# Attention's decay matrices from two triangle scans and a product of two factors, in a fused mLSTM, MoE and MLP kernel on one core

## The chip, the core and the metric

The kernel runs on one core of a Trainium2 chip. A core has five engines, each with an instruction queue of its own, worked off in order: TensorE (PE, with its weight load PEld), VectorE (DVE), ScalarE (ACT), GpSimd (POOL) and SyncE (SP, which here issues DMAs). SBUF is the on-chip memory of 128 partitions, PSUM the accumulators that PE writes. The metric is the device time of one execution in microseconds; lower is better.

## The reference

Three layers follow each other. The first is a gated linear attention (mLSTM) over 4 batches, 8 heads, 768 tokens and a head size of 40; its output, 3072 tokens of 320 values, goes through a mixture of 8 experts with one expert per token, and then through a dense layer of 2048.

```python
for t in range(S):
    m_new = np.maximum(f_gate[:, :, t] + m, i_gate[:, :, t])
    f_stab = np.exp(f_gate[:, :, t] + m - m_new)
    i_stab = np.exp(i_gate[:, :, t] - m_new)
    C = f_stab[:, :, None, None] * C + i_stab[:, :, None, None] * np.einsum('bhd,bhe->bhde', vt, kt)
    n = f_stab[:, :, None] * n + i_stab[:, :, None] * kt
    y[:, :, t] = o * np.einsum('bhde,bhe->bhd', C, qt) / np.maximum(np.abs(nq), 1.0)
```

Only the attention is touched. Over a chunk of tokens it equals a product of scores with a decay matrix whose element (s, t) is the product of `f_stab` from s+1 to t, for s up to t, and zero below.

## The kernel before

The attention is cut into 24 units: 6 chunks of 128 tokens, and in each chunk the 4 batches; unit u is batch u % 4 of chunk u // 4. For every unit and all 8 heads together the kernel builds the decay matrix `pm` (128 source tokens in the partitions, 8 x 128 target tokens in the columns). `fload` (L264) brings the gates of the unit's 8 heads to all partitions with one broadcast DMA from a buffer in DRAM, `scan` (L358) runs one DVE scan over 1024 columns that multiplies by the gates and adds an identity. PE computes the scores (`scores_mm`, L392), DVE multiplies them with `pm` into `wm` (`scores_w`, L402), PE multiplies `wm` with the weighted values (`pv`, L453) and the query with the running state (`inter`, L438), and updates the state (`state`, L407) from keys that POOL weighs with the last column of `pm` (`kweigh`, L383). `epilogue1` and `epilogue2` (DVE) and `finish` (POOL) make the unit's output `x`. Each `pv` pass writes 128 columns, of which the next head overwrites 64, so only 41 per head are used.

The units are pipelined by hand: the loop from L829 on issues, for each u, pieces of several units in a fixed order, and each engine's queue takes them in that order. In iteration u stand, one after the other: `finish(u-2)`, `fload(u+2)`, `scores_mm(u)`, `state_up(u-1)`, `epilogue1(u-1)`, `scan(u+1)`, ranks of a routing batch, `scores_w(u)`, halves of expert weights that are split for later (from u = 10 or 11 on), `pv(u-1)`, `epilogue2(u-1)`, `vprime(u+1)`, `kweigh(u+1)`, the transposes of the output of unit u-2 (`route_t`), `sigm`, `state(u)`, `inter(u)`, the router's logits of unit u-2 (`route_l`, whose last step is a copy on DVE), every fourth unit the router's choice (`route_hot`, five DVE steps), one unit later its counts (`route_cnt`), `state_decay(u)`, scatters of finished rows (POOL; one from u = 10, two from u = 19), and the loads for unit u+3. The scores have one PSUM buffer `sp`, so `scores_mm(u+1)` waits until `scores_w(u)` has read it. `route_t` and a few others share two PSUM buffers named `pt`.

The gates are prepared with 32 partitions (batch and head) by 768 tokens: `gates_m` to `gates_e` (L273 to L317) for chunks 0 and 1 before the loop, and for chunks 2 to 5 spread over units 0 to 5; `put_dec` writes them to DRAM for the broadcasts. `gates_e` makes `est`, the products up to a chunk's last token, which `gates_pe` transposes at unit 5.

Of the kernel before, what the change touches and what calls it, by code (L numbers as in the profile page):

```python
# [9 lines left out]
F32 = mybir.dt.float32  # L10
# [16 lines left out]
def kernel(ctx, tc, qT_in, kT_in, kvo_in, i_gate, f_gate, expert_emb, tau, w12, wio, out, dbg=None):  # L27
# [113 lines left out]
    with ExitStack() as actx:  # L141
# [53 lines left out]
        nc.vector.tensor_copy(ident_h, ident.unsqueeze(1).to_broadcast([P, H, P]))  # L195
        tri = ap1.tile([P, P], F32, name="tri")
# [48 lines left out]
        mm = ap1.tile([BH, S + 1], F32, name="mm")  # L245
# [12 lines left out]
        dec = [dram.tile([n, BH, P], F32, name=f"dec{i}") for i, n in enumerate((2, NCH - 2))]  # L258

        def put_dec(i):  # L260
            c0, c1 = (0, 2) if i == 0 else (2, NCH)
            nc.sync.dma_start(out=dec[i].rearrange("c k t -> k c t"), in_=fz[:, c0:c1])

        def fload(u):  # L264
            b, c = units[u]
            fb[u] = wk.tile([P, H, P], F32, tag="fb", name="fb")
            src = dec[0][c] if c < 2 else dec[1][c - 2]
            src = src[b * H:(b + 1) * H].rearrange("h t -> (h t)").unsqueeze(0)
            nc.sync.dma_start(out=fb[u].rearrange("p h t -> p (h t)"), in_=src.to_broadcast([P, H * P]))
# [1361 lines left out]
```

## Time and profile before

| | |
|---|---|
| three runs | 756.64, 758.26 (median), 759.30 us |
| the profiled execution | 759.01 us, span of its instructions 757.3 us |
| busy over the span | PE 712.0 us (94%), PEld 669.0, DVE 538.7 (71%), ACT 345.2 (46%), POOL 232.4 (31%) |
| granted TensorE clock | 0.99 of full speed over the span |
| attention loop | about the first 180 us; the experts and the dense layer follow |

The page cuts the span into 40 slices of 19 us and gives the busy tenths of each engine: DVE is at 7 to 9 in slices 1 to 11, which are the attention, and at 4 to 7 behind them, where PE is at 9 throughout. The shares of the whole span are an average over stages with different limits.

### The profile page before, as it was taken

Reading aid. Unit: us, or ns where it says so; the run is one execution under the profiler, and the core shown is the slowest. Engines: PE = TensorE matmul, PEld = TensorE weight load, DVE = VectorE, ACT = ScalarE, POOL = GpSimd, SP = SyncE. Lnnn points to the kernel's source line nnn. Section 1 sums busy time; section 2 is a strip of 40 time slices with the busy share of each in tenths; the row PEclk is TensorE's granted clock in tenths of the full one; section 3 lists DMA queues with packets and bytes.
Section 4 is the critical chain, followed back from the end, with each engine's and each line's share of the span. In section 5 each row is a group of like instructions: output and inputs, shape, how many; then the busy total and the mean of one; then the engine's idle time right before and its main releaser. Section 6 shows DMA issues by size and latency. Waiting matters only on the chain.

```text
span 757.3 us, 13220 instructions
## 1 busy us (share of the span) xinstructions
PE 712.0 (94%) x4708; PEld 669.0 (88%) x4708; DVE 538.7 (71%) x1082; ACT 345.2 (46%) x806; POOL 232.4 (31%) x346
## 2 busy tenths in 40 slices
PE   7697888878999999999999999999999999999995
PEld 6697888878888999999998888998889988899994
DVE  7889999998499989898976765544544554445542
ACT  4344243332566666676645443333333343334442
POOL 4563476785343333455401003003003003002011
PEclk9889999999999999999999999999999999999998
DMA  6979887672559777877732121211211101101000
GB/s 188 314 244 300 265 268 237 205 256 77 165 198 234 234 203 188 233 209 232 250 82 80 27 59 46 42 33 40 40 41 36 37 26 35 43 1 46 11 19 18
DMA packets 69913, 99.57 MB, mean 131 GB/s; under 512 B 31218, under 2 KB 56082, under 8 KB 69842
## 3 DMA queue, kind: packets, MB, share of 16 engines
q1 hardware_dynamic: 66770, 90.79, 40.6%
q0 software_dynamic: 3072, 7.89, 2.9%
q8 instruction: 38, 0.62, 0.3%
q14 instruction: 33, 0.27, 0.1%
HBM read 77.53 MB, written 17.19 MB: 125 GB/s over the span
## 4 chain that ended last, share of the span: by engine, by line
issue 42%; PE 23%; POOL 5%; DVE 2%; DMA 1%; ACT 0%; POOLq 0%; SPq 0%; ACTq 0%
PE acc L1131 12%; PE hp L138 10%; POOL out_dram L1176 3%; POOL xr L1282 2%; PE xt L1055 1%; DMA xr<-y 1%; DVE w L121 0%; POOL gap L1178 0%; DVE hs L1105 0%; DVE xl L1057 0%; DVE w L111 0%; DVE fr L1200 0%; POOLq L1626 0%; DVE xl L1073 0%; ACT hs L1444 0%
## 5 line engine op out<-in xcount | busy, mean ns | idle before, releaser
L1131 PE MATMUL acc<-wout,hhl 128*128 128x320 f32 x1152 | 187.0, 309 | 0.0
L1131 PEld LDWEIGHTS acc<-wout,hhl 128*128 128x128 f32 x1152 | 175.9, 188 | 7.4
L1116 DVE TENSOR_TENSOR sg<-hp,sg 128x512 f32<-128x512 f32 (+1 forms) x112 | 68.8, 614 | 93.5 <-ACT sg L1115 93.1
L138 PE MATMUL hp<-xh,win 128*128 128x512 f32 (+1 forms) x560 | 131.0, 364 | 0.0
L1118 DVE TENSOR_TENSOR hhl<-sg,hhl 128x512 fp32r<-128x512 f32 (+1 forms) x112 | 71.3, 637 | 70.2 <-ACT hhl L1117 70.2
L1176 POOL DMA_INDIRECT out_dram<-o,tokd x24 | 24.0, 1001 | 312.4 <-ACT o L1160 308.7
L1115 ACT ACTIVATE sg<-hp 128x512 f32<-128x512 f32 (+1 forms) x112 | 60.4, 539 | 124.6 <-PE hp L138 124.6
L1131 PE MATMUL acc<-w,hs 128*128 128x320 f32 x636 | 104.9, 310 | 2.0 <-ACT hs L1104 1.0
L138 PEld LDWEIGHTS hp<-xh,win 128*128 128x128 f32 x560 | 93.9, 188 | 11.5 <-ACT xh L1321 0.2
L1131 PEld LDWEIGHTS acc<-w,hs 128*128 128x128 f32 x636 | 96.8, 188 | 4.4 <-DVE hs L1105 1.9
L1117 ACT CAST hhl<-sg 128x512 fp32r<-128x512 f32 (+1 forms) x112 | 62.6, 559 | 80.1 <-DVE sg L1116 80.1
L138 PE MATMUL hp<-xl,win 128*128 128x512 f32 (+1 forms) x336 | 85.7, 363 | 0.0
L110 POOL TENSOR_TENSOR w<-r,w 128x256 fp32r<-128x256 f32 x58 | 47.7, 824 | 106.6 <-ACT w L105 94.2
L138 PEld LDWEIGHTS hp<-xl,win 128*128 128x128 f32 x336 | 58.8, 189 | 10.9 <-DVE xl L1322 0.2
L138 PE MATMUL hp<-xh,w 128*128 128x440 f32 (+6 forms) x320 | 66.8, 338 | 0.0
L400 PE MATMUL sp<-qT,kblk 120*128 120x128 f32 x384 | 51.9, 292 | 11.9 <-DVE wm L405 11.9
L400 PEld LDWEIGHTS sp<-qT,kblk 120*128 120x128 f32 x384 | 48.2, 204 | 16.7 <-DVE wm L405 14.6
L360 DVE TENSOR_TENSOR_SCAN pm<-fb,ident_h 128x1024 f32<-128x1024 f32 x23 | 57.3, 2492 | 5.2 <-DMA fb<-dec 2.0
L138 PEld LDWEIGHTS hp<-xh,w 128*128 128x128 f32 x320 | 51.4, 189 | 1.7
L1104 ACT ACTIVATE hs<-hp 128x440 fp32r<-128x440 f32 (+6 forms) x64 | 30.2, 472 | 41.5 <-PE hp L138 40.1
L463 PE MATMUL op<-vp_in,wm 128*128 128x128 f32 (+1 forms) x368 | 44.6, 275 | 0.0
L463 PEld LDWEIGHTS op<-vp_in,wm 128*128 128x128 f32 x368 | 43.5, 194 | 0.0
(304 smaller groups left out, 1082.8 us busy)
## 6 DMA issues: line engine op xcount, KB each, us to landing
r<-in_w_dram SPq DMA_DIRECT2D x32, 704.0 KB
fb<-dec SPq DMA_DIRECT2D x23, 512.0 KB
kvo<-in_kvo_dram SPq DMA_DIRECT2D x24, 480.0 KB
c<-in_wio_dram SPq DMA_DIRECT2D x16, 704.0 KB
rows<-zt SPq DMA_DIRECT2D x8, 640.0 KB
qT<-in_qT_dram SPq DMA_DIRECT2D x24, 180.0 KB
xr<-y SPq DMA_DIRECT2D x5, 640.0 KB
kblk<-in_kT_dram SPq DMA_DIRECT2D x48, 60.0 KB
```

The lines of the kernel that those rows point to most:

```text
L110: eng.tensor_tensor(out=t[:, 3 * P:5 * P].rearrange("p (c f) -> p c f", c=2), in0=r1[:, 0:2], in1=hif[:, 0:2], op=ALU.subtract)
L138: nc.tensor.matmul(hp, a, b, start=(i == 0), stop=(i == len(seq) - 1))
L360: nc.vector.tensor_tensor_scan(out=pm[u].rearrange("p h t -> p (h t)"), data0=fb[u].rearrange("p h t -> p (h t)"), data1=ident_h.rearrange ...
L400: nc.tensor.matmul(sp[:, h - hs.start], kblk[u % NLD][0:KR, h // 3, h % 3, :], qT[u][0:KR, h // 3, :], start=True, stop=True)
L463: nc.tensor.matmul(ops[:, h * NW:h * NW + n], wm[u][:, h], vp_in[u % NLD][:, h * DV:h * DV + n], start=True, stop=True)
L1104: nc.scalar.activation(out=hh, in_=hp, func=AF.Relu)
L1115: nc.scalar.activation(out=sg, in_=hp, func=AF.Sigmoid, scale=1.702)
L1116: nc.vector.tensor_tensor(out=g, in0=hp, in1=sg, op=ALU.mult)
L1117: nc.scalar.copy(hh, g)
L1118: nc.vector.tensor_tensor(out=hl, in0=g, in1=hh.bitcast(F32), op=ALU.subtract)
L1131: nc.tensor.matmul(acc_t[blk][i], hl if j == 2 else hh, w[:, DM:2 * DM] if j == 1 else w[:, 0:DM], start=(first and j == 0), stop=(last an ...
L1176: sc = nc.gpsimd.indirect_dma_start(out=out, out_offset=bass.IndirectOffsetOnAxis(ap=tokd[:, ti:ti + 1], axis=0), in_=o[:, i], in_offset=None)
```

## The change

From chunk 2 on (units 8 to 23) a decay matrix is made of three parts: two triangles of 64x64 tokens for each head, and the square between them. The triangles come from one DVE scan over 512 columns, in which partitions 0 to 63 hold the gates of a chunk's first half and partitions 64 to 127 those of its second half, loaded by two broadcasts of half the width. The scan writes a PSUM buffer `pt`; ACT copies the upper triangle to `pm`. The square is, for each head, an outer product: the products of gates from a source token to the end of the first half, times those from the start of the second half to the target token. `far_mm` forms it for all heads with one PE product over 96 rows, into the upper half of the same PSUM buffer, and `far_out` copies square and lower triangle to `pm` with one ACT copy of 512 columns. `kweigh(u+1)` moves behind `far_out(u+1)` for these units.

The factors are made once for chunks 2 to 5: `factors` inside `gates_e` and `suffix` at the end of iteration 4 (six doubling steps on DVE), `spread_b` and `spread_a` in iterations 5 and 6 (12 ACT products that place each head's or batch's rows among zeros), `masks` in iteration 1. Each factor is split into a rounded part and a rest, which is why the gates lie three times in the partitions: 96 rows, loaded by six DMAs in place of two. `pv` writes 96 columns per pass in place of 128, for all units. The two `pm` buffers become fixed tiles, and an early buffer of the experts takes a `wm` buffer instead.

```diff
-        ig = ap1.tile([BH, S], F32, name="ig")
-        fg = ap1.tile([BH, S], F32, name="fg")
-        nc.sync.dma_start(out=fg, in_=f_gate.rearrange("b h s -> (b h) s"))
-        nc.sync.dma_start(out=ig, in_=i_gate.rearrange("b h s -> (b h) s"))
+        R3, HP, CH = 3 * BH, P // 2, 2
+        ig = ap1.tile([R3, S], F32, name="ig")
+        fg = ap1.tile([R3, S], F32, name="fg")
+        for t, g in ((fg, f_gate), (ig, i_gate)):
+            for a in range(3):
+                nc.sync.dma_start(out=t[a * BH:(a + 1) * BH], in_=g.rearrange("b h s -> (b h) s"))
...
+        id2 = ap1.tile([P, H, HP], F32, name="id2")
+        hmask = ap1.tile([R3, H], F32, name="hmask")
+        bmask = ap1.tile([R3, B], F32, name="bmask")
+        fac = {n: ap1.tile([R3, NCH - CH, HP], F32R, name=n) for n in ("fa", "fb")}
+        facA = ap1.tile([R3, NCH - CH, HP], F32, name="facA")
+        lhsA = ap1.tile([R3, B, NCH - CH, HP], F32R, name="lhsA")
+        rhsB = ap1.tile([R3, NCH - CH, H, HP], F32R, name="rhsB")
+        pmb = [ap1.tile([P, H, P], F32, name=f"pmb{i}") for i in range(2)]
...
-        mm = ap1.tile([BH, S + 1], F32, name="mm")
+        mm = ap1.tile([R3, S + 1], F32, name="mm")
...
-        dec = [dram.tile([n, BH, P], F32, name=f"dec{i}") for i, n in enumerate((2, NCH - 2))]
+        dec = [dram.tile([CH, BH, P], F32, name="dec0"), dram.tile([2 * (NCH - CH), BH, HP], F32, name="dec1")]
...
+            if i == 0:
+                nc.sync.dma_start(out=dec[0].rearrange("c k t -> k c t"), in_=fz[0:BH, 0:CH])
+            else:
+                nc.sync.dma_start(out=dec[1].rearrange("c k t -> k c t"),
+                                  in_=fz[0:BH, CH:NCH].rearrange("k c (a t) -> k (c a) t", t=HP))
...
+            fb[u] = wk.tile([P, H, P], F32, tag="fb", name="fb").rearrange("p h t -> p (h t)")
+            if c < CH:
+                src = dec[0][c, b * H:(b + 1) * H].rearrange("h t -> (h t)").unsqueeze(0)
+                nc.sync.dma_start(out=fb[u], in_=src.to_broadcast([P, H * P]))
+            else:
+                fb[u] = fb[u][:, 0:H * HP]
+                for a in range(2):
+                    src = dec[1][2 * (c - CH) + a, b * H:(b + 1) * H].rearrange("h t -> (h t)").unsqueeze(0)
+                    nc.sync.dma_start(out=fb[u][a * HP:(a + 1) * HP], in_=src.to_broadcast([HP, H * HP]))
...
+            if c0 >= CH:
+                at = lambda t: t.rearrange("k c (a t) -> k c a t", t=HP)[:, c0:c1, :, 0:1]
+                nc.vector.tensor_copy(at(fd), at(fz))
+                nc.vector.memset(at(fz), 0.0)
+                return
...
         def gates_e(c0, c1):
 
             nc.vector.tensor_tensor_scan(out=fl(est, c0, c1), data0=fl(fz, c0, c1), data1=fl(fd, c0, c1), initial=0.0,
                                          op0=ALU.mult, op1=ALU.add)
             n = c1 - c0
+            if c0 >= CH:
+                factors()
             gd = wk.tile([BH, n, B * G], F32, tag="gd", name="gd")
             gd_t[c0] = gd
             nc.vector.tensor_tensor(out=gd, in0=pairm.unsqueeze(1).to_broadcast([BH, n, B * G]),
-                                    in1=est[:, c0:c1, P - 1:P].to_broadcast([BH, n, B * G]), op=ALU.mult)
+                                    in1=est[0:BH, c0:c1, P - 1:P].to_broadcast([BH, n, B * G]), op=ALU.mult)
...
+        def masks():
+
+            v = ident[0:R3, 0:R3].rearrange("k (a b h) -> k a b h", b=B, h=H)
+            nc.vector.tensor_reduce(out=hmask, in_=ident[0:R3, 0:R3].rearrange("k (a h) -> k h a", h=H), axis=AX.X, op=ALU.add)
+            nc.vector.tensor_reduce(out=bmask, in_=v.rearrange("k a b h -> k b a h"), axis=AX.XY, op=ALU.add)
+            for a in range(2):
+                nc.vector.tensor_copy(id2[a * HP:(a + 1) * HP],
+                                      ident[a * HP:(a + 1) * HP, a * HP:(a + 1) * HP].unsqueeze(1).to_broadcast([HP, H, HP]))
+
+        def suffix():
+
+            nc.vector.memset(facA[:, :, HP - 1:HP], 1.0)
+            nc.vector.tensor_copy(facA[:, :, 0:HP - 1], fz[:, CH:NCH, 1:HP])
+            k = 1
+            while k < HP:
+                nc.vector.tensor_tensor(out=facA[:, :, 0:HP - k], in0=facA[:, :, 0:HP - k], in1=facA[:, :, k:HP], op=ALU.mult)
+                k *= 2
+            nc.scalar.copy(fac["fa"], facA)
+            lo = slice(BH, 2 * BH)
+            nc.vector.tensor_tensor(out=fac["fa"][lo], in0=facA[lo], in1=fac["fa"][lo].bitcast(F32), op=ALU.subtract)
+
+        def factors():
+
+            late = est[:, CH:NCH, HP:P]
+            nc.scalar.copy(fac["fb"], late)
+            lo = slice(2 * BH, R3)
+            nc.vector.tensor_tensor(out=fac["fb"][lo], in0=late[lo], in1=fac["fb"][lo].bitcast(F32), op=ALU.subtract)
+            nc.vector.tensor_tensor(out=late, in0=late, in1=est[:, CH:NCH, HP - 1:HP].to_broadcast([R3, NCH - CH, HP]), op=ALU.mult)
+
+        def spread_a():
+            for b in range(B):
+                nc.scalar.mul(lhsA[:, b], fac["fa"].bitcast(F32), bmask[:, b:b + 1])
+
+        def spread_b(h0, h1):
+            for h in range(h0, h1):
+                nc.scalar.mul(rhsB[:, :, h], fac["fb"].bitcast(F32), hmask[:, h:h + 1])
...
         def scan(u):
-            pm[u] = wk.tile([P, H, P], F32, tag="pm", name="pm")
-            nc.vector.tensor_tensor_scan(out=pm[u].rearrange("p h t -> p (h t)"), data0=fb[u].rearrange("p h t -> p (h t)"),
+            pm[u] = pmb[u % 2]
+            if units[u][1] >= CH:
+                t = tri_t[u] = ps_t.tile([P, H, HP], F32, tag="pt", name="tri")
+                nc.vector.tensor_tensor_scan(out=t.rearrange("p h t -> p (h t)"), data0=fb[u], data1=id2.rearrange("p h t -> p (h t)"),
+                                             initial=0.0, op0=ALU.mult, op1=ALU.add)
+                nc.scalar.copy(pm[u][0:HP, :, 0:HP], t[0:HP])
+                return
+            nc.vector.tensor_tensor_scan(out=pm[u].rearrange("p h t -> p (h t)"), data0=fb[u],
                                          data1=ident_h.rearrange("p h t -> p (h t)"), initial=0.0, op0=ALU.mult, op1=ALU.add)
 
+        tri_t = {}
+
+        def far_mm(u):
+            b, c = units[u]
+            if c >= CH:
+                nc.tensor.matmul(tri_t[u][0:HP].rearrange("p h t -> p (h t)"), lhsA[:, b, c - CH],
+                                 rhsB[:, c - CH].rearrange("k h t -> k (h t)"), start=True, stop=True)
+
+        def far_out(u):
+            if units[u][1] >= CH:
+                nc.scalar.copy(pm[u][:, :, HP:P], tri_t.pop(u))
...
-                n = min(2, H - h) * NW
+                n = NW + NW // 2 if h < H - 1 else NW
                 nc.tensor.matmul(ops[:, h * NW:h * NW + n], wm[u][:, h], vp_in[u % NLD][:, h * DV:h * DV + n], start=True, stop=True)
...
-                for n, tag in (("h", "fb"), ("l", "pm")):
+                for n, tag in (("h", "fb"), ("l", "wm")):
...
                 if ok(u - 1):
                     pv(u - 1)
                     epilogue2(u - 1)
+                if ok(u + 1):
+                    far_mm(u + 1)
                 if u == 5:
                     gates_pe(2, NCH)
+                    spread_b(0, H // 2)
+                if u == 6:
+                    spread_b(H // 2, H)
+                    spread_a()
+                if u == 1:
+                    masks()
                 if ok(u + 1):
                     vprime(u + 1)
-                    kweigh(u + 1)
+                    if units[u + 1][1] < CH:
+                        kweigh(u + 1)
...
+                if ok(u + 1) and units[u + 1][1] >= CH:
+                    far_out(u + 1)
+                    kweigh(u + 1)
...
                     gates_e(2, NCH)
                     sigm(u)
+                    suffix()
```

## Rows read from the trace of the kernel before

**Rows 1.** busy time by stretch: us, then PE, PEld, DVE, ACT, POOL, PEclk, DMA, GB/s
```profile
64.60:93.60 29.00, 25.22 (x224) 24.28 (x224) 27.85 (x65) 9.63 (x34) 12.65 (x18) 1.00 0.83 269
93.60:122.70 29.10, 25.07 (x224) 24.20 (x223) 28.36 (x60) 10.75 (x37) 20.17 (x25) 1.00 0.74 238
122.70:151.80 29.10, 24.79 (x221) 23.92 (x220) 28.36 (x60) 10.76 (x37) 20.17 (x25) 1.00 0.75 235
151.80:173.60 21.80, 16.29 (x144) 15.50 (x143) 21.23 (x39) 6.09 (x21) 19.60 (x23) 1.00 0.67 229
```

**Rows 2.** timeline of DVE, one plain interval: start us, us, engine, line, operation
```profile
129.41 2.78 DVE L360 TENSOR_TENSOR_SCAN pm<-fb,ident_h 128x1024 f32<-128x1024 f32 x1
132.12 1.19 DVE L405 TENSOR_TENSOR wm<-sp,pm 128x1024 f32<-128x1024 f32 x1
...
134.76 0.12 DVE L542 COPY logit_all<-r 128x8 f32<-128x8 f32 x1
134.79 0.85 DVE L435 SCALAR_TENSOR_TENSOR Cst<-dC,mask,Cst 120x123 f32<-120x123 f32 x3
...
135.96 2.79 DVE L360 TENSOR_TENSOR_SCAN pm<-fb,ident_h 128x1024 f32<-128x1024 f32 x1
```

**Rows 3.** timeline of PE, the same stretch; in brackets idle before, releaser
```profile
130.12 0.31 PE L507 MATMUL pr<-ident,x 128*128 128x128 f32 x1
...
130.49 0.73 PE L414 MATMUL dC<-vp_in,kw 128*120 128x123 f32 x6
131.06 0.83 PE L450 MATMUL ip<-Cst,qT 120*128 120x123 f32 x6
...
132.21 0.39 PE L540 MATMUL r<-enT,xT 128*128 128x128 f32 x2
133.36 2.05 PE L400 MATMUL sp<-qT,kblk 120*128 120x128 f32 x16 [0.77 <-DVE wm L405]
```

**Rows 4.** groups by line, DVE, up to 60 us: xcount | busy us, mean ns
```profile
L373 DVE TENSOR_TENSOR_SCAN pm<-f,ident_h 128x512 f32<-128x512 f32 x2 | 2.3, 1194 | 0.0
```

**Rows 5.** groups by line, ACT, whole run, one shape
```profile
L1104 ACT ACTIVATE hs<-hp 128x512 fp32r<-128x512 f32 x8 | 4.8, 598 | 8.1 <-PE hp L138 8.1
```

**Rows 6.** timeline of PE in the last part: passes of 256 columns
```profile
702.23 0.75 PE L138 MATMUL hp<-xh,win 128*128 128x256 f32 x5
702.82 0.52 PE L138 MATMUL hp<-xl,win 128*128 128x256 f32 x3
```

**Rows 7.** timeline of ACT, the stretch of group 2
```profile
130.69 0.48 ACT L511 COPY xT<-pr 128x384 f32<-128x384 f32 x1 [4.58 <-PE pr L509]
```

**Rows 8.** timeline of POOL, the stretch of group 2
```profile
129.25 0.81 POOL L501 TENSOR_TENSOR x<-num,sg 128x320 f32<-128x320 f32 x1
130.01 2.71 POOL L380 TENSOR_TENSOR vp_in<-kvo,ei_tok 128x320 f32<-128x320 f32 x1
132.68 0.73 POOL L387 TENSOR_TENSOR kw<-kvo,pm 128x320 f32<-128x320 f32 x1
133.56 1.07 POOL L616 DMA_INDIRECT rows<-x,slot_i  x1 [0.16 <-issue]
```

**Rows 9.** timeline of DVE: a routing choice, from its first step to the step behind
```profile
83.90 0.19 DVE L560 TENSOR_REDUCE mx<-logit_all 128x4 f32<-128x32 f32 x1
...
85.61 0.84 DVE L435 SCALAR_TENSOR_TENSOR Cst<-dC,mask,Cst 120x123 f32<-120x123 f32 x3
```

**Rows 10.** groups by line, DVE, 64.6 to 173.6 us
```profile
L598 DVE TENSOR_TENSOR cnt<-cnt,cs 128x8 bf16<-128x8 bf16 x4 | 2.9, 713 | 0.1
```

**Rows 11.** timeline of SP: one DMA issue
```profile
1.28 0.41 SPq L156 DMA_DIRECT2D ig<-in_i_gate_dram  x1
```

**Rows 12.** groups by line, DVE, 90 to 245 us, a product of 192 columns
```profile
L1243 DVE TENSOR_TENSOR t<-logit_all,rn 128x192 f32<-128x192 f32 x1 | 0.4, 357 | 0.0
```

**Rows 13.** timeline of DVE: the scan of unit 7
```profile
56.13 2.29 DVE L360 TENSOR_TENSOR_SCAN pm<-fb,ident_h 128x1024 f32<-128x1024 f32 x1 [1.30 <-POOL vp_in L380]
```

**Rows 14.** timeline of PE: the scores of unit 4
```profile
37.29 3.79 PE L400 MATMUL sp<-qT,kblk 120*128 120x128 f32 x16 [3.33 <-DVE wm L405]
```

More of the change, by code (lines that the diff above doesn't have):

```diff
@@ L248 @@
         nc.vector.memset(f0, 0.0)
-        fd = ap1.tile([BH, NCH, P], F32, name="fd")
+        fd = ap1.tile([R3, NCH, P], F32, name="fd")
         nc.gpsimd.memset(fd, 0.0)
-        est = ap1.tile([BH, NCH, P], F32, name="est")
+        est = ap1.tile([R3, NCH, P], F32, name="est")
         fz = fg.rearrange("k (c t) -> k c t", t=P)
@@ L256 @@
         gd_t = {}
-        dec = [dram.tile([n, BH, P], F32, name=f"dec{i}") for i, n in enumerate((2, NCH - 2))]
+        dec = [dram.tile([CH, BH, P], F32, name="dec0"), dram.tile([2 * (NCH - CH), BH, HP], F32, name="dec1")]
         def put_dec(i):
-            c0, c1 = (0, 2) if i == 0 else (2, NCH)
-            nc.sync.dma_start(out=dec[i].rearrange("c k t -> k c t"), in_=fz[:, c0:c1])
+            if i == 0:
[3 more added lines that the diff above has]
+                                  in_=fz[0:BH, CH:NCH].rearrange("k c (a t) -> k (c a) t", t=HP))
         def fload(u):
             b, c = units[u]
[L266 to L269, printed above, removed]
+            fb[u] = wk.tile([P, H, P], F32, tag="fb", name="fb").rearrange("p h t -> p (h t)")
[7 more added lines that the diff above has]
+                    nc.sync.dma_start(out=fb[u][a * HP:(a + 1) * HP], in_=src.to_broadcast([HP, H * HP]))
         fl = lambda t, c0, c1: t[:, c0:c1].rearrange("k c t -> k (c t)")
@@ L306, in gates_z @@
             if c0 == 0:
-                nc.vector.tensor_copy(f0[0:BH], fz[:, 0])
+                nc.vector.tensor_copy(f0[0:BH], fz[0:BH, 0])
         def gates_e(c0, c1):
@@ L323, in gates_pe @@
             for i in range(n):
-                nc.tensor.transpose(pg[:, 2 * i * BH:(2 * i + 1) * BH], ist[:, c0 + i], ident[0:BH, 0:BH])
-                nc.tensor.transpose(pg[:, (2 * i + 1) * BH:(2 * i + 2) * BH], est[:, c0 + i], ident[0:BH, 0:BH])
+                nc.tensor.transpose(pg[:, 2 * i * BH:(2 * i + 1) * BH], ist[0:BH, c0 + i], ident[0:BH, 0:BH])
+                nc.tensor.transpose(pg[:, (2 * i + 1) * BH:(2 * i + 2) * BH], est[0:BH, c0 + i], ident[0:BH, 0:BH])
             g0 = 2 * n * BH
@@ L358, in scan @@
         def scan(u):
-            pm[u] = wk.tile([P, H, P], F32, tag="pm", name="pm")
-            nc.vector.tensor_tensor_scan(out=pm[u].rearrange("p h t -> p (h t)"), data0=fb[u].rearrange("p h t -> p (h t)"),
-                                         data1=ident_h.rearrange("p h t -> p (h t)"), initial=0.0, op0=ALU.mult, op1=ALU.add)
+            pm[u] = pmb[u % 2]
[6 more added lines that the diff above has]
+            nc.vector.tensor_tensor_scan(out=pm[u].rearrange("p h t -> p (h t)"), data0=fb[u],
+                                         data1=ident_h.rearrange("p h t -> p (h t)"), initial=0.0, op0=ALU.mult, op1=ALU.add)
+        tri_t = {}
[7 more added lines that the diff above has]
+                nc.scalar.copy(pm[u][:, :, HP:P], tri_t.pop(u))
         def scan0(j):
             if j == 0:
-                pm[0] = wk.tile([P, H, P], F32, tag="pm", name="pm")
+                pm[0] = pmb[0]
             n = H // 2
```

## Prediction

> **What bounds the kernel now.** I began with the 40 slices of the page, to see where VectorE (DVE) is full: in the attention loop, and not behind it. Then I cut the loop at the starts of its scans [rows 1]. The 16 units from chunk 2 on are units 8 to 23; between the scan of unit 8 (64.6 us) and that of unit 23 (173.6 us) lie 15 intervals, 29.0, 29.1 and 29.1 us for four units each and 21.8 us for the last three. DVE is busy 27.9 to 28.4 of each 29 us, TensorE (PE) some 25, ScalarE (ACT) 10 to 11. So DVE sets the pace there. One plain interval shows it: from scan to scan 6.55 us, without a gap on DVE [rows 2], while PE's next scores wait 0.77 us for DVE's product `wm` [rows 3], which leaves PE with 6.55 - 0.77 = 5.78 us of work. Everything behind the loop follows the loop's end, so a microsecond there is a microsecond of the total.
>
> **The change in the loop.** Removed from DVE: a full scan, 2.78 us in the unit shown [rows 2], becomes one of half the length. A scan of 128x512 took 1.19 us [rows 4]; it read PSUM and wrote SBUF, the new one does the reverse, and I take the same. DVE's plain interval falls to about 6.55 - (2.78 - 1.19) = 4.96 us, so DVE no longer sets the pace. The load of `fb` is halved too; it has landed long before it is used in these units, so I count nothing.
>
> Added: on ACT two copies out of PSUM of 512 columns, 0.60 us each [rows 5]; ACT has 18 us of 29 free. On PE one product of 512 columns: five of 256 columns start within 0.59 us [rows 6], 0.12 each, so 0.23. PE gets time back, since `pv` multiplies 96 columns in place of 128 in 14 of its 16 passes: the six state passes (four of 123 columns, two of 82) take 0.57 us from their start to the next step's, the transposes of 128 columns about 0.11 each [rows 3], so a pass of 82 costs about 0.07 and one of 96 about 0.08; 14 x 0.03 = 0.4. PE's own work becomes 5.78 + 0.23 - 0.4 = 5.6 us.
>
> What matters more is a new ring. `far_mm(u+1)` stands in PE's queue before `route_t`, and waits for ACT's first copy, which waits for the scan of u+1; behind it on PE wait the transposes, `state`, `inter` and `route_l`; DVE's copy of the logits waits for `route_l`, and the next scan is queued behind that copy, `state_up` and `epilogue1`. Before, the scan was followed by nothing that PE waited for at once. Its length: `route_t` to the end of `route_l`, 130.12 to 132.60, is 2.48 [rows 3]; logits copy to scan, 134.76 to 135.96, is 1.20 [rows 2]; scan 1.19; copy 0.60; product 0.23; three hand-overs of 0.05 (as `wm`'s end, 133.31, to the scores at 133.36) 0.15. Sum 5.85 us.
>
> GpSimd (POOL) has a ring as well, because `kweigh(u+1)` now waits for ACT's second copy. From `route_t`: the copy of `xT` starts 0.57 later and takes 0.48 [rows 7], then the second copy 0.60, so `kweigh` starts at about 1.75 and takes 0.73; the scatter and what lies around it 1.3; then the two products of `finish` begin at about 3.8, just when the scan does (2.48 + 0.05 + 1.20 = 3.73). A scan and a product of POOL, both of which read SBUF, did not run together: a product that began inside a scan took 2.71 us, the one ahead of it 0.81, and it ended 0.5 us after the scan [rows 8]. If the first product is ahead, the scan starts up to 0.6 us late and the ring is 6.3 to 6.45; if the scan is ahead, `x` is ready 1.19 + 1.6 us after 3.73, at 6.5, and `route_t` waits for it. Bounds 5.85 and 6.55; I take 6.4, nearer the upper end, as two of the three cases lie there.
>
> The Trainium skill, "SBUF — State Buffer", section "Who interferes with whom", says of a DVE instruction with two inputs in SBUF and a GpSimd instruction that reads SBUF that whoever is first holds the shared port for its whole instruction, and the other stops. The 2.71 us agree. By that rule a plain interval would be 6.3 to 6.55; if the two shared the port's bandwidth without stopping it would be about 5.85.
>
> The 15 intervals then: a plain unit 6.4 (6.55 before). A unit with the routing's choice carries 1.71 us more on DVE inside the ring [rows 9], so 5.85 + 1.71, about 7.5; it has no port conflict left, since the scan comes after `finish`. A unit with counts carries up to 0.2 + 0.71 [rows 10], so 6.7. Four units: 2 x 6.4 + 7.5 + 6.7 = 27.0, against 29.1: 2.1 saved, twice, 4.2. The first four (29.0) hold one more chain of small steps on DVE, the choice of the first expert, and less plain work of DVE, as no weights are split there yet: the ring gives least there, I take 0.5 (0 to 1.5). In the last three units (21.8) there is no state: the ring loses 0.57 of PE and some 0.8 of DVE (`state_up` [rows 2]) and PE's work falls to 5.0; POOL, with two scatters, 1.6 + 0.7 + 2.6 = 4.9, up to 6.1 where the scan stands between. I take 6.0, 5.6 and 6.8 (choice): 18.4, so 3.4 saved (2 to 5). Unit 23's own shorter scan: 1.1 at most, as half of it goes, PE busy beside it, 0.5. Sum of gains 8.6 us (5 to 12).
>
> **The change ahead of the loop.** Six loads of the gates in place of two: four more issues on SP of 0.41 us [rows 11], so 1.6 us later for the first gates and for the first q, k and v; queued behind them is all that SP issues at the start. Some of it is taken up where SP waits for the gates anyway: 0 to 1.6, I take 0.9. Gates on 96 partitions in place of 32 cost no more per instruction, as their columns are the same. `masks` at unit 1 is four small instructions, about 1.1 us of DVE; unit 4's scan waits for data later anyway; I take 0.2 (0 to 1.1).
>
> `factors` and `suffix` at unit 4 stand in DVE's queue before `state_up(4)`, `epilogue1(4)`, `scores_w(5)` and the scan of unit 6, all of which shift by as much. Nine operations of up to 256 columns, by the row of 192 columns (0.357 us [rows 12]) 0.3 to 0.45 each and 3.4 together, small ones 0.2, and two waits for ACT's copies of the factors, about 0.5 each: 4.6 us (3.0 to 5.5). Before the scan of unit 7 DVE idles 1.30 us now [rows 13]; that swallows as much. So 3.3 less a little that PE's order gives back, 3.1 (1.5 to 4.2). ACT's twelve products for `rhsB` and `lhsA` fall into units 5 and 6, where PE waits for DVE by then: nothing. Sum of losses 4.2 us (2 to 7).
>
> While DVE works on this, PE idles about 2.4 us before `inter(5)`. An idle stretch of 3.33 us before the scores of unit 4 was followed by 16 passes in 3.79 us, not 2.05 [rows 14, 3]: 1.7 us lost. No row shows whether 2.4 us is enough for that; 0 to 1.7 is in the range. [...]
>
> **Sum.** The profiled execution took 759.01 us (span 757.3 and 1.7 around it). 759.0 - 8.6 + 4.2 = 754.6. The median of the runs, 758.26, lies 0.75 below the profiled one, so I predict 753.9 us.
>
> **Rivals.** (1) The port is not in the way: plain units 5.85, in all about 3.5 us less, 750.4. For it: the two starts lie 0.1 us apart, and any shift parts them. Against: POOL's work and the scan still add up inside one interval.
> (2) No change that can be measured: the loop gives only 7 us, and the early block takes 6.5, by full start delay and the half clock above; about 758. For it: the only gap of DVE in the stretch that could take up the new work is that of 1.30 us.
> (3) Slower: POOL does both products of `finish` ahead of the scan. The scan then starts at 3.8 + 1.6 = 5.4 after `route_t`, and the ring is 5.4 + 1.19 + 0.6 + 0.23 + 0.1 = 7.5. Four plain units lose 1.1 each against my 6.4, three with counts 0.7, two of the last 0.8: 8.1, so 762. It decides from a mean interval 0.3 us (4.4 / 15) above my figures. For it: the tie; against: after the first product the scan has waited longer.
> (4) The scan into PSUM takes nearly as long as the full one: 1.1 us more in the ring; about 765. Only the 1.19 us stand against it.
>
> **Chances.** Mine 0.48 (its own range 750 to 757), (1) 0.15, (2) 0.20, (3) 0.14, (4) 0.03. About 0.3% (2.3 us) is what this kernel's runs can tell from no change, so faster is below 756.0, slower above 760.5. Faster: 0.43 of mine, all of (1), 0.03 of (2): 0.61. Same: 0.05 and 0.15: 0.20. Slower: (3), (4) and 0.02: 0.19. The range 748 to 761 leaves out the lower half of (1), and most of (3) and (4).
>
> **What would show it.** A half scan of 1.2 us; plain intervals of 6.3 to 6.5 with PE waiting for ACT before `far_mm`, and DVE with gaps before the logits copy; choice units near 7.5; unit 7's scan 2 to 4 us later than 56.1. I am wrong if DVE is still without gaps, if the scans are 7 us apart or 5.9, or if the early units lose over 7 us.

## The result and the profile after

The changed kernel takes 764.88 us (median of four runs, 764.27 to 767.43) where the kernel before takes 758.35 beside it: a ratio of 1.0095 (95% interval 1.0066 to 1.0124), 6.5 us slower. 753.9 was predicted, with 748 to 761 as the range, so it lies outside, on the slower side. The profiled execution is the one of 767.43 us, with a span of 765.7; most of its excess over the median is a stretch at the lower clock, priced below.

The same cuts as in [rows 1], in the profile after, from the scan of unit 8 to that of unit 23:

```profile
70.30:100.60 30.30, 25.58 (x225) 24.40 (x223) 25.16 (x65) 13.86 (x43) 11.60 (x17) 1.00 0.67 210
100.60:132.20 31.60, 27.36 (x216) 26.33 (x215) 25.79 (x60) 15.01 (x45) 20.28 (x26) 0.89 0.63 199
132.20:161.30 29.10, 26.01 (x232) 25.22 (x232) 24.76 (x60) 14.88 (x45) 16.87 (x23) 1.00 0.66 196
161.30:180.70 19.40, 17.66 (x154) 16.77 (x153) 16.34 (x38) 9.36 (x27) 16.77 (x23) 1.00 0.76 230
```

DVE has come down from 28 to 25 us of work per four units, as the change meant, and the stretches are not shorter: 30.3, 31.6 and 29.1 against 29.0, 29.1 and 29.1. Only the last three units gained, 19.4 against 21.8. The first cut begins at 70.3 where it began at 64.6: 5.8 us were lost before the loop. So two things went wrong, and the starts of the scans in DVE's timeline separate them for every kernel run here:

| kernel | us | before beside it | ratio (95%) | scan of unit 6 at | unit 8 | units 8 to 23 |
|---|---|---|---|---|---|---|
| before | | 758.35 | | 50.01 | 64.60 | 108.96 |
| after | 764.88 | 758.35 | 1.0095 (1.0066 to 1.0124) | 56.66 | 70.37 | 110.42 |
| e1 early work alone | 764.66 | 760.02 | 1.0063 (1.0040 to 1.0087) | 56.01 | 69.72 | 109.00 |
| e2 far_mm late | 772.50 | 760.02 | 1.0139 (1.0105 to 1.0173) | 56.10 | 69.81 | 118.06 |
| e3 ACT order | 770.87 | 760.02 | 1.0131 (1.0104 to 1.0157) | 56.37 | 70.08 | 115.61 |
| e4 suffix late | 771.37 | 760.02 | 1.0150 (1.0127 to 1.0173) | 52.59 | 74.59 | 108.72 |
| e5 suffix late, mended | 768.57 | 760.52 | 1.0096 (1.0065 to 1.0126) | 52.35 | 71.01 | 110.69 |
| e6 far_mm late, kweigh late | 755.30 | 760.52 | 0.9915 (0.9887 to 0.9943) | 56.77 | 70.48 | 97.74 |
| e7 e5 and e6 | 756.83 | 760.52 | 0.9945 (0.9928 to 0.9963) | 53.99 | 71.93 | 97.77 |
| e8 PE kept busy | 767.78 | 760.52 | 1.0090 (1.0059 to 1.0120) | 56.78 | 71.53 | 108.08 |
| e9 e6, suffix on POOL | 749.60 | 758.00 | 0.9889 (0.9873 to 0.9905) | 53.13 | 67.33 | 96.60 |
| e10 kweigh late alone | 761.07 | 758.00 | 1.0038 (1.0025 to 1.0051) | 55.90 | 69.60 | 106.43 |
| e11 e6, pv of 128 columns | 753.25 | 758.00 | 0.9934 (0.9915 to 0.9953) | 56.73 | 70.45 | 97.33 |
| e12 e10, far_out late | 762.69 | 758.50 | 1.0056 (1.0034 to 1.0078) | 57.71 | 71.42 | 105.45 |

The ratios are taken over fast runs alone and are not quotients of the medians beside them; one execution of e11, of 2476.17 us, is in its median and not in its ratio. The last three columns come from one profiled execution of each kernel.

**A plain unit after.** DVE, scan to scan, 6.55 us as before:

```profile
138.83 1.22 DVE L424 TENSOR_TENSOR_SCAN tri<-fb,id 128x512 f32<-128x512 f32 x1
...
143.48 0.17 DVE L622 COPY logit_all<-r 128x8 f32<-128x8 f32 x1 [0.75 <-PE r L620]
144.21 0.85 DVE L515 SCALAR_TENSOR_TENSOR Cst<-dC,mask,Cst 120x123 f32<-120x123 f32 x3 [0.56 <-ACT Cst L501]
...
145.38 1.85 DVE L424 TENSOR_TENSOR_SCAN tri<-fb,id 128x512 f32<-128x512 f32 x1
```

PE in the same stretch:

```profile
138.51 1.90 PE L543 MATMUL op<-vp_in,wm 128*128 128x96 f32 x16
140.72 0.45 PE L436 MATMUL tri<-rhsB,lhsA 96*64 96x512 f32 x1 [0.31 <-ACT pmb L426]
141.00 0.28 PE L587 MATMUL pr<-ident,x 128*128 128x128 f32 x1
...
143.06 0.39 PE L620 MATMUL r<-enT,xT 128*128 128x128 f32 x2
```

ACT in the same stretch:

```profile
140.09 0.58 ACT L426 COPY pmb<-tri 64x512 f32<-64x512 f32 x1 [2.12 <-DVE tri L424]
...
141.91 0.59 ACT L441 COPY pmb<-tri 128x512 f32<-128x512 f32 x1
142.38 0.48 ACT L549 ACTIVATE sg<-kvo 128x320 f32<-128x320 f32 x1
...
143.21 0.97 ACT L501 ACTIVATE Cst<-Cst,gdec 120x123 f32<-120x123 f32 x3
```

The half scan takes 1.22 us, as forecast, but DVE now idles twice for others. The ring of the prediction can be walked through the starts: scan 138.83, ACT's copy 140.09, `far_mm` 140.72, `route_t` 141.00, logits copy 143.48 (2.48 from `route_t`, the predicted number), next scan 145.38. Those last 1.90 us were forecast as 1.20. In between DVE waits 0.56 us for `state_decay`, the last row of ACT, which stands in ACT's queue behind `far_out` (141.91), the sigmoid (142.38) and a square that the router needs. So the ring passes through ACT twice: once from the scan to `far_mm`, and once more from the transposes over `far_out` to `state_up` on DVE.

**A unit with the routing's choice** (from the scan at 145.38 to that at 154.49, 9.11 us, forecast 7.5). DVE, and POOL beside it:

```profile
150.66 0.17 DVE L622 COPY logit_all<-r 128x8 f32<-128x8 f32 x1 [0.50 <-PE r L620]
150.86 0.19 DVE L640 TENSOR_REDUCE mx<-logit_all 128x4 f32<-128x32 f32 x1
151.08 0.73 DVE L642 TENSOR_TENSOR vv<-logit_all,mx 128x32 f32<-128x32 f32 x1
151.85 0.68 DVE L644 TENSOR_TENSOR vv<-vv,w 128x32 f32<-128x32 f32 x1
152.57 0.19 DVE L646 TENSOR_REDUCE mx<-vv 128x4 f32<-128x32 f32 x1
152.79 0.61 DVE L648 TENSOR_TENSOR oh_all<-vv,mx 128x32 bf16<-128x32 f32 x1
...
154.49 1.22 DVE L424 TENSOR_TENSOR_SCAN tri<-fb,id 128x512 f32<-128x512 f32 x1
```

```profile
150.68 1.01 POOL L696 DMA_INDIRECT rows<-x,slot_i  x1 [0.16 <-issue]
...
151.74 0.73 POOL L578 TENSOR_TENSOR sg<-sg,dn 128x320 f32<-128x320 f32 x1
152.55 0.80 POOL L581 TENSOR_TENSOR x<-num,sg 128x320 f32<-128x320 f32 x1
```

From the logits copy to the scan 3.83 us, forecast 1.20 + 1.71 = 2.91; the scan that opens this unit, at 145.38, took 1.85. Both excesses stand beside POOL's work: 0.92 and 0.66 (1.85 against the 1.19 forecast) make up the 1.6 us missed. With POOL idle the steps are short: in e5, at unit 6, all five took 0.17 to 0.19 us. The Trainium skill, "SBUF — State Buffer", section "Who interferes with whom", says that a DVE instruction with two SBUF inputs contends with a GpSimd instruction that reads SBUF, and that one with at most one SBUF input, outside the 2-port modes, does not. The trace agrees: the three steps with two inputs are those that stretch here, and the two reductions stay at 0.19.

**The early units.** DVE at unit 4 before the change, then after it, and PE and the windows behind it:

```profile
45.87 1.25 DVE L311 TENSOR_TENSOR_SCAN est<-fg,fd 32x512 f32<-32x512 f32 x1
...
47.72 0.83 DVE L435 SCALAR_TENSOR_TENSOR Cst<-dC,mask,Cst 120x123 f32<-120x123 f32 x3
```

```profile
47.07 1.21 DVE L334 TENSOR_TENSOR_SCAN est<-fg,fd 96x512 f32<-96x512 f32 x1
48.75 0.42 DVE L370 TENSOR_TENSOR fb<-est,fb 32x256 fp32r<-32x256 f32 x1 [0.47 <-ACT fb L368]
49.20 0.92 DVE L371 TENSOR_TENSOR est<-est 96x256 f32<-96x256 f32 x1
...
51.00 2.44 DVE L359 TENSOR_TENSOR facA<-facA 96x252 f32<-96x252 f32 x6
53.91 0.41 DVE L363 TENSOR_TENSOR fa<-facA,fa 32x256 fp32r<-32x256 f32 x1 [0.47 <-ACT fa L361]
54.36 0.85 DVE L515 SCALAR_TENSOR_TENSOR Cst<-dC,mask,Cst 120x123 f32<-120x123 f32 x3
```

```profile
55.36 1.42 PE L494 MATMUL dC<-vp_in,kw 128*120 128x123 f32 x6 [3.58 <-DVE Cst L515]
```

```profile
50.00:55.00 5.00, 1.78 (x18) 1.42 (x16) 4.26 (x14) 2.02 (x8) 0.70 (x1) 0.79 1.02 330
55.00:60.00 5.00, 4.64 (x23) 4.67 (x24) 4.93 (x7) 4.79 (x16) 0.73 (x1) 0.53 0.33 94
...
125.00:130.00 5.00, 4.80 (x22) 4.62 (x23) 3.41 (x8) 3.51 (x12) 2.24 (x4) 0.50 0.03 3
```

The chain from the scan of `est` to `state_up` takes 54.36 - 47.07 = 7.29 us; before it took 1.85 (45.87 to 47.72). That is 5.4 us of block where 4.6 was forecast. It also starts 1.2 us later (47.07 against 45.87). PE idles 3.58 us, and the granted clock falls to 0.53 over the next window, near the 1.2 GHz level: the six state passes take 1.42 us, not 0.73 [rows 3]. The last window is the stretch in the loop that the profiled execution spent at that level.

### The profile page after: what moved, and what is told of

The parts are those of the page before. It is cut to its first block, busy times and chain, and to the rows that moved or that the text cites. A ratio compares the mean times of both kernels' runs of the same rounds, so it can differ in the third digit from the quotient of the medians.

```text
span 765.7 us, 13325 instructions
## 1 busy us (share of the span) xinstructions
PE 719.5 (94%) x4724; PEld 675.8 (88%) x4724; DVE 530.7 (69%) x1097; ACT 367.7 (48%) x852; POOL 231.5 (30%) x346
## 4 chain that ended last, share of the span: by engine, by line
PE 51%; issue 13%; DVE 4%; DMA 1%; POOL 1%; ACT 0%; POOLq 0%; SPq 0%; ACTq 0%
PE hp L138 25%; PE acc L1224 25%; DMA xr<-rows 1%; POOL out_dram L1269 1%; DVE w L121 1%; PE xt L1148 1%; DVE hs L1198 1%; DVE w L111 1%; DVE xl L1150 0%; POOL xr L1375 0%; DVE fr L1293 0%; POOLq L1719 0%; DVE xl L1166 0%; PE xt L1164 0%; ACT w L118 0%
## 5 line engine op out<-in xcount | busy, mean ns | idle before, releaser
L138 PEld LDWEIGHTS hp<-xl,win 128*128 128x128 f32 x336 | 58.9, 189 | 10.9 <-DVE xl L1415 0.2
L543 PE MATMUL op<-vp_in,wm 128*128 128x96 f32 (+1 forms) x368 | 44.3, 274 | 0.0
L138 PE MATMUL hp<-xl,w 128*128 128x440 f32 (+6 forms) x192 | 42.9, 331 | 0.0
```

Source lines behind the costliest of these rows:

```text
L138: nc.tensor.matmul(hp, a, b, start=(i == 0), stop=(i == len(seq) - 1))
L543: nc.tensor.matmul(ops[:, h * NW:h * NW + n], wm[u][:, h], vp_in[u % NLD][:, h * DV:h * DV + n], start=True, stop=True)
```

## The experiments

**e1: the early work alone.** The kernel before with the early part of the change; the factors are computed and not used.

```
 the changed kernel, but
-    far_mm(u + 1), far_out(u + 1); half scan; dec1 in halves; gates_z at every 64th column
+    scan, fload, gates_z, kweigh, pv as before
-    out=late (factors)
+    out=lhsA[:, 0], read by nobody
```

> The kernel before with only the early work of the change: gates on 96 partitions by six loads, the masks, both factors with their logarithmic steps, and their spreading for TensorE, whose results nobody reads. Scans, loads of fb and pv are the old ones; the product of late and the last early value goes to a tile that nobody reads. Theory A (the early work costs as much as the leads in the trace show, +5.8 us at the scan of unit 8, and nothing behind gives it back, because DVE sets the pace of the old loop): 763 to 765 us, scan of unit 8 about 5.5 us later than before. Theory B (the early loss is taken up by a wait further on, and it is the new loop that costs the time): 758 to 760.

764.66 against 760.02: 4.6 us. The scan of unit 8 comes 5.1 us late, and the loop behind it takes 109.00 us as before (108.96). Theory A holds: nothing gives the early loss back. By these numbers 0.0063 of the 0.0095 is early work. The new loop, meant to gain 8.6 us, gained next to nothing: 110.42 us in the profiled execution, and 108.08 in e8, which has the same loop and no stretch at the lower clock in it.

**e2 and e3: the ring.** e3 moves only `far_out` with `kweigh`; e2 moves `far_mm` as well.

```
-    far_mm(u + 1)                   # ahead of route_t      (e2)
-    far_out(u + 1); kweigh(u + 1)   # ahead of sigm         (e2, e3)
     for i in rts[-1:]:
         route_l(i)
+    far_mm(u + 1)                   #                       (e2)
     ...
     state_decay(u)
+    far_out(u + 1); kweigh(u + 1)   #                       (e2, e3)
```

> The changed kernel with far_mm put behind route_l in PE's queue, and far_out with kweigh behind state_decay on ACT and POOL. Theory A (the interval of 6.55 us is a ring: scan, ACT copy, far_mm, route_t to route_l, DVE, with ACT's queue as a second link): without it PE's own work sets the pace, 5.78 + 0.23 = 6.0 us, as pv has not become shorter; plain intervals 5.9 to 6.2, choice units 8.0 to 8.7, in all 6 to 9 us less than the changed kernel, 756 to 759 us. Theory B (DVE's scan against POOL's products sets the interval): plain intervals stay at 6.4 to 6.6, 763 to 765.

> The changed kernel with far_mm where it is, but far_out (and kweigh with it) behind the three steps of state_decay in ACT's queue. Theory A (in a plain unit DVE's state_up waits 0.56 us for state_decay, which stands behind far_out, the sigmoid and the square on ACT): the wait goes down by the 0.59 us of far_out, plain intervals 6.0 to 6.2, 4 to 6 us less than the changed kernel, 759 to 761. Theory B (PE's queue behind far_mm is the longer part of the ring): intervals 6.4 or more, within 2 us of the changed kernel.

Both are slower, 772.50 and 770.87, and neither theory forecast that. In e2 the first two intervals are 6.47 and 6.45 us, without the ring. Behind the first scatter most are 8.1 to 9.6, with 6.76, 5.13 and 7.09 among them. PE in e2, and POOL ahead of it:

```profile
99.40 0.33 PE L587 MATMUL pr<-ident,x 128*128 128x128 f32 x1 [1.87 <-POOL x L581]
...
99.78 1.28 PE L494 MATMUL dC<-vp_in,kw 128*120 128x123 f32 x6
```

```profile
95.76 1.17 POOL L696 DMA_INDIRECT rows<-x,slot_i  x1 [0.20 <-DMA kblk<-in_kT_dram]
...
97.00 1.47 POOL L578 TENSOR_TENSOR sg<-sg,dn 128x320 f32<-128x320 f32 x1
98.54 0.80 POOL L581 TENSOR_TENSOR x<-num,sg 128x320 f32<-128x320 f32 x1
```

`kweigh` now waits for a later `far_out`; the scatter and both products of `finish` stand behind it, PE waits 1.87 us for `x`, and its next passes run at a lower clock (0.68 granted over 100 to 105 us; the state passes take 1.28 us, not 0.73). e3 shows the same:

```profile
105.04 0.47 PE L587 MATMUL pr<-ident,x 128*128 128x128 f32 x1 [1.84 <-POOL x L581]
```

There too the clock falls (0.68 granted over 105 to 110 us). Some of e3's intervals are the 6.2 us of its theory A, but five of the 15 are 8.9 to 10.9. One wait was exchanged for another, and the clock added to its price.

**e4, e5 and e8: the early block on DVE.** e4 and e5 take `suffix` apart; e8 gives PE something to do in the gap.

```
     if u == 4:
-        suffix()
+    if u == 5: suffix(1, 8)                      # e4, e5: three products, end of the unit
+    if u == 6: suffix(8, HP)                     # the others, ahead of route_t; e4: ACT's copy too
+    if u == 6: suffix_lo(); spread_a()           # end of the unit; e5: ACT's copy here
+    if u == 5: keep_warm(r_bank(None), 16)       # e8 alone, behind route_t
```

> The changed kernel with suffix taken apart: three of its six products at the end of unit 5, three in unit 6 where DVE waits for the logits, the subtraction at the end of unit 6. Theory A (these 3.7 us on DVE stand ahead of the scan of unit 6, and PE's 3.6 us of idle time brings the clock down): the scan of unit 6 comes 3.3 to 4 us earlier than in the changed kernel, PE keeps its full clock there, the scan of unit 8 comes 2 to 3.5 us earlier; 761 to 763 us. Theory B (what holds these units up is the late start of the loads): no change, 764 to 765.

> The changed kernel with suffix taken apart as in e4_suffix_late, but ACT's copy of fa at the end of unit 6, behind the copy of xT that route_l waits for (in e4_suffix_late it stood ahead of it and PE waited 6.35 us for xT). Theory A (nine tenths of the early loss is DVE's block at unit 4 and the clock that falls behind it, and e4_suffix_late hid that by its own new wait on ACT): scan of unit 6 about 4 us earlier than in the changed kernel as there (52.6 us), and now kept: scan of unit 8 at 66.5 to 68.5 us against 70.4; 760 to 763 us. Theory B (the work costs the same wherever it stands in these units): scan of unit 8 at 70 or later, 764 to 766.

> The changed kernel with 16 products of the identity with itself put on PE at unit 5 behind route_t, where PE idles 3.58 us while DVE computes the factors. They fill some 3.5 us. Theory A (the lower clock between 55 and 60 us costs PE about 1.7 us, and DVE waits for PE there): the clock stays at its upper level, the scan of unit 8 comes 1 to 2 us earlier, 763 to 764 us. Theory B (DVE's own work sets these units, PE's speed is hidden): the scan of unit 8 comes at the same time within 0.5 us, 764.5 to 765.5.

In e4 the scan of unit 6 came 4.1 us earlier with PE at its full clock, and more than that was lost again by unit 8 (74.59 against 70.37): ACT's copy of `fa` stood ahead of the copy of `xT`, the transposed output that the router's logits are made from. One row of PE in e4 shows it:

```profile
67.53 0.80 PE L622 MATMUL r<-enT,xT 128*128 128x128 f32 x2 [6.35 <-ACT xT L595]
```

e5 mends that and still gains nothing at unit 8 (71.01 against 70.37). Its rows for PE:

```profile
59.81 1.42 PE L497 MATMUL dC<-vp_in,kw 128*120 128x123 f32 x6 [1.82 <-DVE Cst L518]
...
66.55 0.77 PE L621 MATMUL r<-enT,xT 128*128 128x128 f32 x2 [2.74 <-DVE logit_all L625]
```

PE waits for DVE at the two new places instead, 1.82 and 2.74 us, and the clock falls there (0.69 and 0.66 granted over 60 to 70 us). Three products also took 2.65 us beside POOL, not 1.2. Theory B's forecast for unit 8 came true, for this one arrangement on DVE: by then the work had cost as much as where it stood before. e8 settles nothing, and neither theory's time came (767.78): the filler had to wait for ACT's copy `gdec` out of the same PSUM buffer, so PE idled 2.07 us all the same, the clock fell (0.72 over 55 to 60 us), and the filler's 5.4 us at that clock held up the unit.

**e6, e10, e12: what the loop waits for.** In e6 `kweigh(u)` is called a unit later, behind `finish`, with e2's other two moves. e10 is that call alone; e12 adds `far_out` behind `state_decay`.

```
     finish(u - 2, nc.gpsimd)
+    if units[u][1] >= CH: kweigh(u)      # e6, e10, e12; its old call goes
-    far_mm(u + 1)  /  +  behind route_l  # e6 alone
-    far_out(u + 1) /  +  behind state_decay   # e6, e12
```

> The changed kernel with far_mm behind route_l and far_out behind state_decay as in e2_far_late, and kweigh(u+1) moved to the next unit, behind the products of finish in POOL's queue. Theory A (e2_far_late had no ring through far_mm any more, 6.45 us per unit while no scatter was queued, but kweigh, the scatter and finish then stood in one line on POOL behind the late far_out, PE waited 1.7 to 1.9 us for x, and its clock fell): plain intervals 5.9 to 6.3, choice units 6.5 to 7.5, no fall of the clock; 750 to 756 us. Theory B (a port that DVE's scan and POOL's products share costs this wherever they stand): PE still waits over 1 us for x, intervals of 9 us at the lower clock, 765 or more.

> The changed kernel with kweigh(u+1) alone moved to the next unit, behind finish in POOL's queue; far_mm ahead of route_t and far_out stay where the change put them. It tells which of the two edits of e6_pool_order does it. Theory A (the ring through far_mm sets the plain interval: scan, ACT, far_mm, PE, logits, DVE): plain intervals stay at 6.3 to 6.6, at most 2 us gained over the 15 intervals, 764 to 767 us where the kernel before has 760. Theory B (POOL's line of kweigh, scatter and finish alone sets it): intervals of 5.6 to 6.0 as in e6_pool_order, 755 to 757.

> e10_kweigh_only with far_out behind state_decay in ACT's queue; far_mm stays ahead of route_t. In e10_kweigh_only the plain interval is 6.55 us, and DVE idles twice in it: 0.86 us for the logits (PE's queue behind far_mm) and 0.56 us for state_decay's Cst (ACT's queue behind far_out). Theory A (the ring has two links one after the other, and ACT's adds its wait to PE's): without the second one plain intervals 6.0 to 6.1, which is the prediction's ring of 5.85 us and a little; some 4 us less than e10_kweigh_only, about 757 us where the kernel before has 758. Theory B (only PE's queue behind far_mm counts, the second wait would be taken up elsewhere): plain intervals stay at 6.4 to 6.6, within 1.5 us of e10_kweigh_only.

e6 takes 755.30 against 760.52, 0.9915: faster than the kernel before. Its loop takes 97.74 us, 12.7 less than the changed kernel's, of which 2.1 are the lower clock in that one execution. DVE and POOL there, in a plain unit:

```profile
128.99 1.66 DVE L424 TENSOR_TENSOR_SCAN tri<-fb,id 128x512 f32<-128x512 f32 x1
...
133.48 0.17 DVE L622 COPY logit_all<-r 128x8 f32<-128x8 f32 x1 [0.18 <-PE r L620]
...
134.72 1.36 DVE L424 TENSOR_TENSOR_SCAN tri<-fb,id 128x512 f32<-128x512 f32 x1
```

```profile
127.97 0.72 POOL L578 TENSOR_TENSOR sg<-sg,dn 128x320 f32<-128x320 f32 x1 [1.24 <-DVE dn L571]
128.76 0.80 POOL L581 TENSOR_TENSOR x<-num,sg 128x320 f32<-128x320 f32 x1
129.52 1.66 POOL L467 TENSOR_TENSOR kw<-kvo,pmb 128x320 f32<-128x320 f32 x1
```

The interval is 5.73 us; DVE's long waits are gone, and the four plain units in the middle of the loop take 5.55 to 5.78. `x` is ready before PE asks for it, and what runs beside the scan is `kweigh`. That is not free either: `kweigh` ends at 131.18, and PE's state passes, which use its result, start at 131.23, after their weight load has waited 0.4 us for it. The choice units take 7.90, where theory A had 6.5 to 7.5.

e10 says which edit did it. With POOL's line out of the way alone, plain units stay at 6.55, on the same two waits (DVE in e10):

```profile
139.72 0.17 DVE L622 COPY logit_all<-r 128x8 f32<-128x8 f32 x1 [0.86 <-PE r L620]
140.45 0.85 DVE L515 SCALAR_TENSOR_TENSOR Cst<-dC,mask,Cst 120x123 f32<-120x123 f32 x3 [0.56 <-ACT Cst L501]
```

So theory A holds for the plain units. Choice units fell from 9.11 to 8.00: the scan ahead took 1.46 us, not 1.85, and the three steps 0.19, 0.68 and 0.44, not 0.73, 0.68 and 0.61, which makes up the 1.1 us and bears out that POOL had stretched them. The loop took 4.0 us less where I expected 2 at most; but 2.1 of the 4.0 are the lower clock in the changed kernel's execution, and one plain unit of e10 took 8.00 us, of which its scan waited 1.04 for `fb`.

e12 then takes ACT's link away: plain units 6.20 to 6.33, not the 6.0 to 6.1 expected, so the link is real and worth 0.2 to 0.35 of its 0.56 us. Others of its units were longer, one at a lower clock and one by a wait of 1.06 us for `fb`, and its time (1.0056) cannot be told from e10's (1.0038): the expected 757 was not reached. The larger part of the ring is PE's queue behind `far_mm`: e6 differs from e12 in the place of `far_mm` alone, and its plain units are 5.55 to 5.78 and its loop 97.74 us, not 105.45. In the same way e6 differs from e2 in the place of `kweigh` alone (97.74 against 118.06). Neither of the two moves gives this without the other.

**e9 and e7: a version that beats both.** e7 is e5 and e6 together, and its early part spoils it again: 756.83, outside both forecasts, with the scan of unit 8 at 71.93 us, where e6 has it at 70.48. e9 is e6 with `suffix` on POOL.

```
-    nc.vector.tensor_copy / tensor_tensor (facA, fa)
+    nc.gpsimd.tensor_copy / tensor_tensor (facA, fa)
+    if u == 5: suffix_lo()      # ACT's copy of fa and the subtraction, end of the unit
```

> The edits of e5_suffix_late2 and of e6_pool_order together. If both theories A hold, the gains add: 3 us from the early units and 9 to 14 us from the loop, 748 to 753 us, faster than the kernel before. If the loop is bound by something that neither touches, it stays at 758 or above.

> e6_pool_order with the whole of suffix on POOL (its copy, its six products and the subtraction) where it stood on DVE, and ACT's copy of fa and the subtraction at the end of unit 5. POOL idles 4.7 us between 50 and 55 us. Theory A (the early loss is DVE's block at unit 4, and it costs what PE and DVE wait for it; on an idle engine it costs nothing): scan of unit 6 at 52 to 53.5 us, scan of unit 8 at 66 to 68 us against 70.5 in e6_pool_order; 2.5 to 4.5 us less, 751 to 753 us where e6_pool_order has 755.3. Theory B (POOL's products take DVE's port, so that they cost DVE as much as its own): scan of unit 8 at 69.5 or later, 754.5 to 756.

e9: 749.60 against 758.00, 0.9889 (0.9873 to 0.9905), faster than the kernel before and than the changed one. POOL takes twice as long over the six products, and PE keeps its clock (POOL's row, then the window):

```profile
46.81 5.22 POOL L359 TENSOR_TENSOR facA<-facA 96x252 f32<-96x252 f32 x6
```

```profile
55.00:60.00 5.00, 4.70 (x44) 4.54 (x42) 4.90 (x11) 4.67 (x16) 4.84 (x5) 1.00 1.00 305
```

The scan of unit 6 comes at 53.13 and that of unit 8 at 67.33, 3.1 us earlier than in e6 and 2.7 later than in the kernel before. Both are what theory A said. The times alone do not part e9 from e6, as the intervals of their ratios overlap; the two scans do.

**e11: the columns of pv.**

```
-    n = NW + NW // 2 if h < H - 1 else NW
+    n = min(2, H - h) * NW
```

> e6_pool_order with pv's passes back at 128 columns (96 in the change). PE is never idle for long there, so its work is the time. Theory A (a pass takes what its weights of 128 columns take to load, 0.11 us, so that 96 columns saved nothing): intervals and time as in e6_pool_order, within 1 us. Theory B (the prediction's 0.03 us for each of 14 passes): plain intervals longer by 0.4 us, 4 to 6 us more.

Theory A holds: the time (0.9934) and the loop (97.33 us) are e6's. One row of PE from e11, to be held against the 96 columns above:

```profile
121.44 1.90 PE L543 MATMUL op<-vp_in,wm 128*128 128x128 f32 x16
```

The same 1.90 us. The Trainium skill, "TensorE: Matmul & The Clock Gate", section "LDWEIGHTS (loading the stationary operand)", gives the load of weights as about their columns divided by 1.2, in ns, which makes an estimate of 107 for 128 columns. The trace has 1.90 / 16 = 119 ns a pass, with the last one's end in it, and weights of 128 columns in both kernels. That the load sets this pace fits, but no run here changes the weights' columns alone.

## Why the prediction was wrong

The forecast for the 15 intervals was 100.9 us, and the profile has 110.4. Of these 9.5 us the two choice units in the middle are 3.2, the lower clock 2.1, the first four units 1.8, the four plain units in the middle 1.1, the last three 1.0, and the two units with counts 0.3. Another 1.6 us are the early part. Two steps of the prediction's ring failed, the path from the logits to the scan and the choice; the points below name them.

- **What bounded the kernel before:** right for the loop. DVE set the pace; in e6, with the half scan and the ring out of the way, the loop is 11.2 us shorter than before. That DVE is full in the loop alone was misread: the page's row of DVE has 8 and 9 again in slices 12 to 20, behind the loop. PE is at 9 there, and from the scan of unit 23 to the end of the span it took 583.7 us before and 584.9 after, so the misreading did no harm.
- **The half scan:** right, 1.22 us against 1.19. Beside POOL's products it took up to 1.85, 0.63 more, which is about the 0.6 us that the prediction charged for such a meeting as a late start of the scan.
- **The ring:** its links were right one by one (2.48 for PE, 0.6 for the copy), but it was not complete. The step "logits copy to scan is 1.20" failed: it is 1.90, because DVE waits 0.56 us there for `state_decay`. I counted DVE's operations and did not ask which of them waits for ACT's queue, into which the change puts two copies. 6.4 was close to the measured 6.55 by luck, since it was 5.85 and a surcharge for POOL; e10 shows that POOL's order does not set the plain unit.
- **The choice:** "it has no port conflict left, since the scan comes after `finish`" failed. The conflict is on the choice's own steps and on the scan that opens the unit. The unit took 9.1 us instead of 7.5, a loss of 0.4 against 8.70 to 8.72 before instead of a gain.
- **The first four units and the last three:** 30.3 against my 28.5, since small steps on DVE stand inside the ring and `route_slot` waits 0.7 us for a copy that stands behind the new one on ACT; 19.4 against 18.4, where one scan waited 1.17 us for `fb`, to which I had given no cost, as it was to land long before its use.
- **PE's 0.4 us from pv:** did not exist (e11). I took a price per column from passes whose weights were smaller as well.
- **The early part:** mis-sized, 4.2 forecast, 5.8 at unit 8 in the profile and 4.6 to 5.1 in e1, inside my bounds of 2 to 7. The block began 1.2 us late, where 0.9 and 0.2 were forecast for the loads and the masks. The block was 5.4 instead of 4.6, and the clock, left out of the sum, did fall behind a gap of 3.58 us on PE, forecast as 2.4: from `state` to the scores 3.85 us (55.36 to 59.21), where it was 1.95 (50.42 to 52.37).
- **The clock in the loop:** not forecast. In the profiled execution the interval of units 15 to 16 takes 8.97 us with 0.50 granted over 125 to 130 us; in e8, whose loop is the same, 6.87. So 2.1 us of that execution's 110.4 are this, and the forecast had no term for it.
- **The rivals:** the second one named both parts, a loop that gains less and an early block of 6.5. It kept a gain of 7 in the loop, of which next to nothing came. The third had the right sign and a wrong price: in three units POOL's second product did start just ahead of the scan, which then took 1.71 to 1.85 us, 0.5 to 0.6 more and not 1.1, and e10 shows that this is not what sets the plain unit. e2 was slow through POOL as well, but at PE, which waited for `x`, and not at the scan.

Open stays why PE's clock fell behind the gaps of 1.82 and 2.74 us in e5 while a gap of 2.10 us in e9 was followed by 1.00, and what of e9's remaining 2.7 us is the six loads and what the factors.

## What to carry to other kernels

When work leaves the engine that sets the pace, write out the new ring through every queue that it enters, ACT's too, and ask of each instruction behind the new one who waits for it. Put the new instructions behind whatever someone waits for: the same operations were 0.95% slower than the kernel before as they stood, and 0.85% faster when three calls were moved. Work done once goes to the engine that idles, even at twice the price (5.22 us on POOL instead of 2.44 on DVE brought the loop's start 3.1 us forward), since a gap on PE was often paid twice here, as the gap and at the clock behind it.

## What the runs showed that I had not expected

- The granted clock fell after gaps shorter than the 3.33 us of [rows 14]: after 1.87 us in e2, and after three of 0.8 to 1.0 us in the profiled execution of the changed kernel (116 to 125 us); the same three, at 148 to 156 us, were followed by 1.00.
- Two-input steps of 32 columns on DVE, 0.19 us alone, took 0.61 to 0.73 beside POOL. A scan of 512 columns went from 1.22 to 1.85.
- 16 passes on PE, 14 of them of 96 columns or of 128, take the same 1.90 us where the weights have 128.
